# Pairs of heads in half-tiles of 64 partitions, 48 KB runs, three shared buffers

## The chip, the cores and the metric

The kernel runs on one core of one Trainium2 chip. The metric is the device time of one execution in microseconds: the median of three runs of the kernel before is 527.67 us (526.96 to 527.71). A profile of one further execution shows where the time goes.

## The reference

One step of decoding in a transformer block with a parallel feed-forward part: x has 4 rows (batch B = 4, one token each) of D = 640.

```python
def _A_ref(x, k_cache, v_cache, wq, wo):
    W = min(4096, max(256, Sk // 4))                     # Sk = 8192, so W = 2048
    q = (x @ wq).reshape(B, Sq, Hq, Dh).transpose(0, 2, 1, 3)   # 32 heads of 192
    k = k_cache[:, :, Sk - W:, :]
    v = v_cache[:, :, Sk - W:, :]
    scores = jnp.einsum("bhqd,bhkd->bhqk", q, k) * (Dh ** -0.5)
    p = _softmax(scores, axis=-1)
    o = jnp.einsum("bhqk,bhkd->bhqd", p, v)
    return o.transpose(0, 2, 1, 3).reshape(B, Sq, Hq * Dh) @ wo
def _B_ref(x, w1, w3, w2):                               # F = 1536
    return (silu(x @ w1) * (x @ w3)) @ w2
xn = _layernorm(x)
return x + _A_ref(xn, ...) + _B_ref(xn, ...)
```

All arrays are bf16. The last 2,048 positions of K and of V are read for each of 32 heads and 4 batch rows: 2 x 100.7 MB. wq and wo have 7.9 MB each, w1, w3 and w2 2.0 MB each. In all 223 MB are read, each byte once, for one query row per head and batch row.

## The kernel before

**Layout.** A tile of K or V holds one head for all four batch rows. `cache_rows` (L102) cuts the 2,048 positions into NQ = 32 pieces of NJ = 64; partition q*4 + b holds piece q of batch row b, which is one run of 64 x 192 x 2 B = 24 KB in memory. So a tile is 128 partitions x 24 KB, 3 MB, loaded by one DMA (`load_k` L105, `load_v` L110). K and V have three buffers each, 144 KB per partition in all. All large loads are issued by SyncE (SP), in the order in which they are written.

**Scores.** q is made once (L205 to L213) from wq, which is loaded into the V buffers in rows of 24 KB, and spread over the partitions by a matmul with a selector (`q_bcast`, L215). A slot s is half a head, 32 positions per partition. `mult` (L225) multiplies K with q on VectorE, `adder` (L234) sums the 192 products in groups of 16 by 12 identity matmuls that accumulate in PSUM, and `reduce_tile` (L248) finishes the sums on VectorE.

**Softmax and P·V.** The chain runs once for a pair of heads (u): `chain_lmax` takes the maximum of each partition, `chain_tr` transposes, `chain_gmax` takes that of each batch row and head, `chain_bc` spreads it back and ScalarE takes the exponential with its sum; `chain_z` (L288) writes the probabilities into a block form with a column for each batch row. `pv` (L303) does P·V of one head: 8 steps of 8 positions, in each three matmuls for three thirds of the head's 192 columns, with 32 columns of weights each. The result holds the wanted numbers on a diagonal; `pick` (L318) multiplies it with a mask, `pick_sum` (L327) sums it, `fold` (L333) adds the partitions by a small matmul, and ScalarE scales by the reciprocal of the softmax sum into o_bf.

**Output.** For a group of HG = 4 heads `ge_tr` (L346) transposes o_bf and `ge_proj` (L353) multiplies with that group's wo rows, accumulating in one PSUM tile for the whole kernel. A group's wo is one DMA of 0.98 MB in runs of 7.7 KB, double-buffered (`wo_load`, L115). w1, w3 and w2 go into K buffers after the last K (`ffn_load` L363, `w2_load` L368); `ffn_mm` (L375) does gate and up, `ffn_transpose` (L392) brings the product into the form that the last matmuls (L464 to L468) need.

**Order.** Every piece is entered with `add(slot, phase, ...)` (L400), and the pieces are written out sorted by slot and phase (L451). Each engine works in the order in which its instructions are written, apart from what a planner moves; `behind` (L244) holds VectorE's other work behind the multiplication of the same slot. The loads stand in the same list:

```python
        if j >= KBUFS:
            add(NC * j - 3, 0, load_k, j)
        add(NC * j + 2, 8, load_v, j)
        add(NC * j + L, 2, pv, j)
...
        add(a + 2 if not last else end, 10, wo_load, hg)
```

A load waits on SP until its buffer is free, and what is written behind it on SP waits with it.

Of the kernel before, what the change touches and what calls it, by code (L numbers as in the profile page):

```python
# [10 lines left out]
FP32 = mybir.dt.float32  # L11
# [7 lines left out]
def kernel(  # L19
# [14 lines left out]
    HG: int = 4,  # L34
    QP: int = 8,
    KBUFS: int = 3,
    VBUFS: int = 3,
    PBUFS: int = 2,
    L: int = 7,
    ALIGN: int = 144,  # L40
):

# [12 lines left out]
    NQ = P // B  # L55
    NJ = W // NQ
    NC = NJ // CH
    NK = Dh // DD
    SCALE = float(Dh) ** -0.5
    EPS = 1e-5  # L60
    MASK = -30000.0
    NS = H * NC
    HH = 2
    PL = 32 // B
    DV = 512 // PL
    NV = Dh // DV
    RPP = (HG * Dh) // P
    OW = HG * Dh
    NCH = 512
    QW = 512  # L70
    QB = QP * Dh // QW
    FC = F // P
    DH = D // 2
    assert NJ % CH == 0 and CH * DD <= 512 and QP * Dh % QW == 0
    assert OW % P == 0 and Dh % RPP == 0 and H % HG == 0 and HG % HH == 0 and H % QP == 0 and QP % HH == 0
    assert NV * 32 <= P and NJ % (2 * PL) == 0 and DV * NV == Dh
# [3 lines left out]
    NB = H * Dh // QW // NG  # L80
    assert H * Dh % (QW * NG) == 0 and NB <= 3
    assert DH <= 512 and F % NCH == 0 and NF <= NG

    const = ctx.enter_context(tc.tile_pool(name="const", bufs=1))
    kpool = ctx.enter_context(tc.tile_pool(name="kt", bufs=KBUFS))
    vpool = ctx.enter_context(tc.tile_pool(name="vt", bufs=VBUFS))
    wpool = ctx.enter_context(tc.tile_pool(name="wstream", bufs=2))
    ppool = ctx.enter_context(tc.tile_pool(name="pr", bufs=PBUFS))
    qpool = ctx.enter_context(tc.tile_pool(name="qbc", bufs=2))
    opool = ctx.enter_context(tc.tile_pool(name="o", bufs=2))  # L90
    small = ctx.enter_context(tc.tile_pool(name="small", bufs=3))
# [5 lines left out]
    kts, vts, prs, pss, scs, zts = {}, {}, {}, {}, {}, {}  # L97
    qbcs, wos, o_pss, rss, rcps, o_rs, o_bfs, chs = ({} for _ in range(8))
    mult_insts, es, o_ms = {}, {}, {}
    ORDER_DEP = mybir.DependencyInfo(mybir.DependencyClass.NoSync, mybir.DependencyReason.SCHED_ONLY)  # L100

    def cache_rows(cache, h):  # L102
        return cache[:, h, Sk - W:Sk, :].rearrange("b (q n) d -> q b (n d)", q=NQ)

    def load_k(j):  # L105
        kt = kpool.tile([P, NJ, Dh], BF16, tag="kt")
        nc.sync.dma_start(out=kt[:], in_=cache_rows(A_k_cache, j))
        kts[j] = kt

    def load_v(j):  # L110
        vt = vpool.tile([P, NJ, Dh], BF16, tag="vt")
        nc.sync.dma_start(out=vt[:], in_=cache_rows(A_v_cache, j))  # L112
        vts[j] = vt

    def wo_load(hg):  # L115
        wt = wpool.tile([P, RPP * D], BF16, tag="w")
        nc.sync.dma_start(out=wt[:], in_=A_wo[hg * OW:(hg + 1) * OW, :].rearrange("(p i) n -> p (i n)", i=RPP))
        wos[hg] = wt

    x_sb = ppool.tile([B, D], BF16, tag="pr")  # L120
    x_rows = A_x.rearrange("b s d -> (b s) d")
    nc.scalar.dma_start(out=x_sb[:], in_=x_rows)
# [7 lines left out]
    RV = NJ * Dh // (H * Dh)  # L130
    wq_rows = A_wq.rearrange("(p kc) n -> p kc n", kc=KC)
    wqs = []
    for r0 in range(0, KC, RV):
        r1 = min(r0 + RV, KC)
        wt = vpool.tile([P, RV, H * Dh], BF16, tag="vt")
        nc.sync.dma_start(out=wt[:, 0:r1 - r0, :], in_=wq_rows[:, r0:r1, :])  # L136
        wqs.append(wt)
    for h in range(KBUFS):
        load_k(h)
# [6 lines left out]
    nc.vector.memset(pad[:, 0:1], 0.0)  # L146
    nsc = const.tile([HH, HH], FP32, name="nsc")
    nc.vector.tensor_scalar_mul(out=nsc[:], in0=idf[0:HH, 0:HH], scalar1=-SCALE)
    selm = const.tile([P, B], FP32, name="selm")
    nc.vector.tensor_reduce(out=selm[:], in_=idf[:].rearrange("p (q b) -> p b q", b=B), axis=AX.X, op=ALU.add)  # L150
    selb = const.tile([P, B], BF16, name="selb")
    nc.vector.tensor_copy(out=selb[:], in_=selm[:])
    row = const.tile([P, 32], FP32, name="row")
    nc.vector.tensor_reduce(out=row[:], in_=idf[:].rearrange("p (g c) -> p c g", g=NG), axis=AX.X, op=ALU.add)
    fsel = const.tile([P, NV, B], FP32, name="fsel")
    nc.vector.tensor_reduce(out=fsel[:], in_=idf[:, 0:NV * 32].rearrange("p (k l b) -> p k b l", k=NV, l=PL), axis=AX.X, op=ALU.add)
    diag = const.tile([P, HH, PL], FP32, name="diag")
    for hh in range(HH):
        nc.vector.tensor_reduce(out=diag[:, hh, :], in_=row[:].rearrange("p (l b) -> p l b", b=B), axis=AX.X, op=ALU.add)
    oTs = []  # L160
    for i in range(2):
        oT = const.tile([P, RPP, 32], BF16, name=f"oT{i}")
        nc.gpsimd.memset(oT[:], 0.0)
        oTs.append(oT)

    xf = ppool.tile([B, D], FP32, tag="pr")
    nc.vector.tensor_copy(out=xf[:], in_=x_sb[:])
    ssum = const.tile([B, 1], FP32, name="ssum")
    nc.vector.tensor_reduce(out=ssum[:], in_=xf[:], axis=AX.X, op=ALU.add)
    negmean = const.tile([B, 1], FP32, name="negmean")  # L170
    nc.vector.tensor_scalar_mul(out=negmean[:], in0=ssum[:], scalar1=-1.0 / D)
    xc = ppool.tile([B, D], FP32, tag="pr")
    nc.vector.tensor_scalar_add(out=xc[:], in0=xf[:], scalar1=negmean[:, 0:1])
    ssq = const.tile([B, 1], FP32, name="ssq")
    nc.scalar.activation(out=xf[:], in_=xc[:], func=ACTF.Square, accum_out=ssq[:])
# [6 lines left out]
    xn = ppool.tile([B, D], BF16, tag="pr")  # L182
    nc.vector.tensor_scalar_mul(out=xn[:], in0=xc[:], scalar1=rstd[:, 0:1])

    xnT_ps = ps_t.tile([P, KC, B], BF16, tag="t")
    for kc in range(KC):
        nc.tensor.transpose(out=xnT_ps[:, kc, :], in_=xn[:, kc:D:KC], identity=idb[0:B, 0:B])
# [3 lines left out]

    sel = const.tile([P, NQ, B], BF16, name="sel")
    nc.vector.tensor_copy(out=sel[:], in_=selm[:].unsqueeze(1).to_broadcast([P, NQ, B]))

# [3 lines left out]
    for k in range(NB):  # L198
        if k < 2:
            qp = ps_add.tile([P, QW], FP32, tag="ps")  # L200
        else:
            qt = ps_o.tile([P, HH, QW], FP32, tag="o_ps")
            qp = qt[:, 0, :]
        q_pss.append(qp)
    for kc in range(KC):  # L205
        for k in range(NB):
            for g in range(NG):
                off = (k * NG + g) * QW
                nc.tensor.matmul(q_pss[k][32 * g:32 * g + 32, :], lhsT=xnT[:, kc, :],  # L209
                                 rhs=wqs[kc // RV][:, kc % RV, off:off + QW], start=(kc == 0), stop=(kc == KC - 1))  # L210
    q_sb = const.tile([P, NB, QW], BF16, name="q_sb")
    for k in range(NB):
        nc.scalar.copy(out=q_sb[:, k, :], in_=q_pss[k][:, :])  # L213

    def q_bcast(qg, m):  # L215
        k, g = (qg * QB + m) // NG, (qg * QB + m) % NG
        if m == 0:
            qbc = qpool.tile([P, QP, Dh], BF16, tag="qbc")
            qbcs[qg] = qbc
        bp = ps_t.tile([P, QW], FP32, tag="t")  # L220
        nc.tensor.matmul(bp[:], lhsT=sel[32 * g:32 * g + B].rearrange("k q b -> k (q b)"),  # L221
                         rhs=q_sb[32 * g:32 * g + B, k, :], start=True, stop=True)
        nc.scalar.copy(out=qbcs[qg][:].rearrange("p h d -> p (h d)")[:, m * QW:(m + 1) * QW], in_=bp[:])  # L223

    def mult(s):  # L225
        j, c = s // NC, s % NC
        pr = ppool.tile([P, CH, Dh], BF16, tag="pr")
        mi = nc.vector.tensor_tensor(out=pr[:], in0=kts[j][:, c * CH:(c + 1) * CH, :],  # L228
                                     in1=qbcs[j // QP][:, j % QP, :].unsqueeze(1).to_broadcast([P, CH, Dh]),
                                     op=ALU.mult)  # L230
        prs[s] = pr
        mult_insts[s] = mi

    def adder(s):  # L234
        ps = ps_add.tile([P, CH, DD], FP32, tag="ps")
        pr = prs.pop(s)
        for kk in range(NK):
            nc.tensor.matmul(ps[:], lhsT=idb[:], rhs=pr[:, :, kk * DD:(kk + 1) * DD],  # L238
                             start=(kk == 0), stop=(kk == NK - 1))
        pss[s] = ps  # L240

    slot = [0]

    def behind(inst):  # L244
        if slot[0] in mult_insts:
            tc.add_manual_dep(inst.ins, mult_insts[slot[0]].ins.name, ORDER_DEP, reason="vector engine issue order")

    def reduce_tile(s):  # L248
        j, c = s // NC, s % NC
        if s % (HH * NC) == 0:  # L250
            sc = small.tile([P, HH, NJ], FP32, tag="sc", bufs=2)
            scs[j // HH] = sc
        ri = nc.vector.tensor_reduce(out=scs[j // HH][:, j % HH, c * CH:(c + 1) * CH], in_=pss.pop(s)[:], axis=AX.X, op=ALU.add)  # L253
        behind(ri)

    def chain_lmax(u):
        lmax = small.tile([P, HH], FP32, tag="lmax")
        behind(nc.vector.tensor_reduce(out=lmax[:], in_=scs[u][:], axis=AX.X, op=ALU.max))  # L258
        chs[u] = [lmax]
# [43 lines left out]
    def pv(j):  # L303
        u, hh = j // HH, j % HH
        if hh == 0:
            o_ps = ps_o.tile([P, HH, PL * DV], FP32, tag="o_ps")
            o_pss[u] = o_ps
# [196 lines left out]
```

## Time and profile before

| | |
|---|---|
| median of the runs | 527.67 us |
| the profiled execution | 526.79 us |
| its span, first to last instruction | 525.0 us |
| busy: TensorE, VectorE, ScalarE | 326.4, 328.3, 39.6 us |
| main DMA queue | 222.97 MB, 99.0% of 16 engines' span |
| granted TensorE clock, mean | 0.844 |

The page divides the span into 40 slices of 13.1 us; a digit is the busy share of a slice in tenths. "Idle before" of a group of instructions is the idle time of its engine just ahead of them, with what ended it. The chain of waits is followed back from the last instruction. In the timeline, a line gives start and length in us, then engine, line, operation, output and inputs, and how many. PEld is TensorE's loading of weights, which overlaps its matmuls. Matmuls that write different columns of the array run beside each other, so their mean lengths don't add up.

### The profile page before, as it was taken

Reading aid. Unit: us, or ns where it says so; the run is one execution under the profiler, and the core shown is the slowest. Engines: PE = TensorE matmul, PEld = TensorE weight load, DVE = VectorE, ACT = ScalarE, POOL = GpSimd, SP = SyncE. Lnnn points to the kernel's source line nnn. Section 1 sums busy time; section 2 is a strip of 40 time slices with the busy share of each in tenths; the row PEclk is TensorE's granted clock in tenths of the full one; section 3 lists DMA queues with packets and bytes.
Section 4 is the critical chain, followed back from the end, with each engine's and each line's share of the span. In section 5 each row is a group of like instructions: output and inputs, shape, how many; then the busy total and the mean of one; then the engine's idle time right before and its main releaser. Section 6 shows DMA issues by size and latency. Waiting matters only on the chain.

```text
span 525.0 us, 4658 instructions
## 1 busy us (share of the span) xinstructions
PE 326.4 (62%) x1991; PEld 142.2 (27%) x1991; DVE 328.3 (63%) x289; ACT 39.6 (8%) x121; POOL 1.8 (0%) x11
## 2 busy tenths in 40 slices
PE   2356376864758487662858566572857737585864
PEld 1122122321323133221324223231322313232432
DVE  3069455767757376865757486573758657575842
ACT  2300000100000010001000000100100000000121
POOL 1000000000000000000000000000000000000000
PEclk9999887786888778797878769797897868888889
DMA  8999999999999999999999999999999999999996
GB/s 360 433 436 428 431 436 426 438 426 433 431 432 432 433 434 427 436 429 429 439 424 434 429 435 426 438 422 439 434 430 429 430 434 434 430 433 430 426 428 256
DMA packets 11723, 223.25 MB, mean 425 GB/s; under 512 B 1316, under 2 KB 1464, under 8 KB 2872
## 3 DMA queue, kind: packets, MB, share of 16 engines
q1 hardware_dynamic: 11688, 222.97, 99.0%
q8 instruction: 15, 0.25, 0.2%
q14 instruction: 4, 0.03, 0.0%
q10 hardware_dynamic: 16, 0.01, 0.0%
HBM read 222.96 MB, written 0.01 MB: 425 GB/s over the span
## 4 chain that ended last, share of the span: by engine, by line
DMA 77%; DVE 13%; PE 8%; SPq 1%; issue 0%; DVEq 0%
DMA kt<-in_A_k_cache_dram 73%; DVE pr L228 11%; PE ps L238 6%; DMA w2t<-in_B_w_dram 5%; PE o_ps L313 1%; DVE sc L253 1%; SPq L112 0%; DVE o_r L331 0%; SPq L136 0%; DVE o_m L323 0%; PE acc L357 0%; SPq L372 0%; PE ft L467 0%; DVE z L291 0%; DVE res L470 0%
## 5 line engine op out<-in xcount | busy, mean ns | idle before, releaser
L238 PE MATMUL ps<-pr,idb 128*128 128x512 bf16 x768 | 223.7, 452 | 166.3 <-DVE pr L228 166.3
L228 DVE TENSOR_TENSOR pr<-kt,qbc 128x6144 bf16<-128x6144 bf16 x64 | 214.5, 3352 | 166.8 <-DMA kt<-in_A_k_cache_dram 166.8
L238 PEld LDWEIGHTS <-idb 128*128 128x128 bf16 x768 | 83.9, 112 | 285.1 <-issue 223.9
L313 PE MATMUL o_ps<-vt,z 128*32 128x512 bf16 x768 | 66.3, 389 | 1.2 <-DMA vt<-in_A_v_cache_dram 0.6
L253 DVE TENSOR_REDUCE sc<-ps 128x32 f32<-128x512 f32 x64 | 43.7, 683 | 6.8 <-PE ps L238 6.7
L313 PEld LDWEIGHTS <-z 128*32 128x32 bf16 x768 | 32.0, 98 | 28.3 <-issue 10.5
L331 DVE TENSOR_REDUCE o_r<-o_m 96x128 f32<-96x1024 f32 (+1 forms) x17 | 30.7, 1807 | 0.1
L283 ACT ACTIVATE e<-sc,negm 128x64 bf16<-128x64 f32 x32 | 10.9, 340 | 239.4 <-DVE negm L279 239.4
L323 DVE TENSOR_TENSOR o_m<-o_ps,diag 96x1024 f32<-96x1024 f32 (+1 forms) x17 | 19.5, 1148 | 7.6 <-PE o_ps L313 7.6
L344 ACT ACTIVATE o_bf<-fp,rcp 4x192 bf16<-4x192 f32 x32 | 11.4, 403 | 132.0 <-PE fp L338 132.0
L338 PE MATMUL fp<-o_r,fsel 96*4 96x128 f32 x96 | 13.1, 273 | 1.8 <-DVE o_r L331 1.8
L223 ACT CAST qbc<-bp 128x512 bf16<-128x512 f32 x12 | 6.8, 590 | 81.2 <-PE bp L221 81.2
L291 DVE TENSOR_TENSOR z<-e,selb 128x512 bf16<-128x512 bf16 x16 | 10.8, 678 | 0.9 <-ACT e L283 0.9
L209 PE MATMUL qp<-wt,xnT 128*32 128x512 bf16 x40 | 5.3, 623 | 8.2 <-DMA wt<-in_A_wq_dram 8.2
L338 PEld LDWEIGHTS fp<-o_r,fsel 96*4 96x4 f32 x96 | 7.1, 86 | 9.8 <-issue 5.5
L357 PE MATMUL acc<-wt,oT 128*32 128x320 bf16 x96 | 7.9, 301 | 0.8 <-DVE oT L351 0.8
L263 PE MATMUL mt<-idf,lmax 128*2 128x128 f32 x16 | 4.8, 301 | 5.5 <-DVE lmax L258 5.4
L277 PEld LDWEIGHTS mt<-nsc,gmq 2*128 2x128 f32 x32 | 4.7, 183 | 7.8 <-issue 6.4
L277 PE MATMUL mt<-nsc,gmq 2*128 2x2 f32 x32 | 6.1, 257 | 1.1 <-DVE gmq L271 1.1
L283 ACT ACTIVATION_READ_ACCUMULATOR e<-sc,negm 128x1 f32 x32 | 6.0, 187 | 0.0
L209 PEld LDWEIGHTS <-xnT 128*32 128x32 bf16 x60 | 2.4, 133 | 11.9 <-issue 11.0
L263 PEld LDWEIGHTS mt<-idf,lmax 128*2 128x2 f32 x16 | 1.3, 83 | 13.8 <-issue 8.1
(65 smaller groups left out, 69.9 us busy)
## 6 DMA issues: line engine op xcount, KB each, us to landing
kt<-in_A_k_cache_dram SPq DMA_DIRECT2D x32, 3072.0 KB, 34.3
vt<-in_A_v_cache_dram SPq DMA_DIRECT2D x32, 3072.0 KB, 32.4
wt<-in_A_wo_dram SPq DMA_DIRECT2D x8, 960.0 KB, 26.4
wt<-in_A_wq_dram SPq DMA_DIRECT2D x2, 3072.0 KB
wt<-in_B_w_dram SPq DMA_DIRECT2D x2, 1920.0 KB, 20.5
wt<-in_A_wq_dram SPq DMA_DIRECT2D x1, 1536.0 KB, 19.9
w2t<-in_B_w_dram SPq DMA_DIRECT2D x2, 640.0 KB
w2t<-in_B_w_dram SPq DMA_DIRECT2D x1, 480.0 KB
```

The costliest lines, as they stand in the source:

```text
L228: mi = nc.vector.tensor_tensor(out=pr[:], in0=kts[j][:, c * CH:(c + 1) * CH, :], in1=qbcs[j // QP][:, j % QP, :].unsqueeze(1).to_broadcast ...
L238: nc.tensor.matmul(ps[:], lhsT=idb[:], rhs=pr[:, :, kk * DD:(kk + 1) * DD], start=(kk == 0), stop=(kk == NK - 1))
L253: ri = nc.vector.tensor_reduce(out=scs[j // HH][:, j % HH, c * CH:(c + 1) * CH], in_=pss.pop(s)[:], axis=AX.X, op=ALU.add)
L277: nc.tensor.matmul(mt[:, P:P + HH], lhsT=gmq[:].rearrange("o q b -> o (q b)"), rhs=nsc[:], start=True, stop=True)
L283: nc.scalar.activation(out=e[:, hh, :], in_=sc[:, hh, :], func=ACTF.Exp, bias=negm[:, hh:hh + 1], scale=SCALE, accum_out=rs[:, hh:hh + 1])
L291: behind(nc.vector.tensor_tensor(out=z[:].rearrange("p h j b -> p (h j) b"), in0=e[:].rearrange("p h j -> p (h j)").unsqueeze(2).to_broadc ...
L313: nc.tensor.matmul(o_ps[32 * k:32 * k + 32, hh, :], lhsT=z[:, hh, g * PL:(g + 1) * PL, :].rearrange("p l b -> p (l b)"), rhs=vt[:, g * PL: ...
L323: behind(nc.vector.tensor_tensor(out=o_ms[u][:, h0:h1].rearrange("r h l d -> r (h l) d"), in0=o_pss[u][0:NV * 32, h0:h1, :].rearrange("r h ...
L331: behind(nc.vector.tensor_reduce(out=o_rs[u][:, h0:h1, :], in_=o_ms[u][:, h0:h1].rearrange("r h l d -> r h d l"), axis=AX.X, op=ALU.add))
L338: nc.tensor.matmul(fp[:, :, k * DV:(k + 1) * DV], lhsT=fsel[0:NV * 32, k, :], rhs=o_r[:], start=True, stop=True)
L344: nc.scalar.mul(out=o_bfs[hg][:, pr + hh, :], in_=fp[:, hh, :], mul=rcp[:, hh:hh + 1])
L357: nc.tensor.matmul(acc[32 * t:32 * t + 32, :], lhsT=oT[:, i, :], rhs=wo_t[:, i * D + t * DH:i * D + (t + 1) * DH], start=(hg == 0 and i == ...
```

## The change

A unit u is now a pair of heads (X = 2), 16 units in all. The 2,048 positions are cut into NQ = 16 pieces of NJ = 128, so a partition holds one run of 128 x 192 x 2 B = 48 KB. The first head of the pair lies in partitions 0 to 63, the second in 64 to 127; each half is loaded by its own DMA of 3 MB (`load`). A K or V tile is 6 MB, and there are three such buffers that K, V, the first four fifths of wq, and later w1, w3 and w2 together use in turn.

A unit has four slots, as two heads had before, with the same multiplications and identity matmuls. The softmax chain and everything behind it runs once per unit, as before once per pair. P·V has 64 columns of weights: 16 steps; the first two thirds of the columns are two matmuls beside each other into one PSUM bank (`pv(u, 0)`), the last third goes alternately to two halves of the second bank (`pv(u, 1)`). The output weights come in groups of 8, 8, 8, 4 and 4 heads, in runs of 15 KB for the groups of eight, into one buffer that the last two groups share; the transposes before the projection are matmuls with a selector, which also adds the two half-rows. w2 is loaded in runs of 10, 3.8 and 1.3 KB. VectorE and TensorE now follow the written order completely (`dve`, `pe`).

```diff
-    KBUFS: int = 3,
-    VBUFS: int = 3,
-    PBUFS: int = 2,
+    GS: tuple = (8, 8, 8, 4, 4),
     L: int = 7,
...
-    NQ = P // B
+    X = 2
+    HP = P // X
+    NQ = HP // B
...
-    kpool = ctx.enter_context(tc.tile_pool(name="kt", bufs=KBUFS))
-    vpool = ctx.enter_context(tc.tile_pool(name="vt", bufs=VBUFS))
-    wpool = ctx.enter_context(tc.tile_pool(name="wstream", bufs=2))
+    kvpool = ctx.enter_context(tc.tile_pool(name="kv", bufs=3))
+    wpool = ctx.enter_context(tc.tile_pool(name="wstream", bufs=1))
...
+    def load(cache, u):
+        kv = kvpool.tile([P, NJ, Dh], BF16, tag="kv")
+        for x in range(X):
+            nc.sync.dma_start(out=kv[x * HP:(x + 1) * HP],
+                              in_=cache[:, X * u + x, Sk - W:Sk, :].rearrange("b (q n) d -> q b (n d)", q=NQ))
+        return kv
...
+    def wo_load(g):
+        n = GS[g] * Dh // P
+        if g < len(GS) - 1:
+            wt = wpool.tile([P, GM * Dh // P * D], BF16, tag="w")
+            wos["tile"] = wt
+        at = 0 if g < len(GS) - 1 else GS[-2] * Dh // P * D
+        wos[g] = wos["tile"][:, at:at + n * D]
+        nc.sync.dma_start(out=wos[g], in_=A_wo[starts[g] * Dh:(starts[g] + GS[g]) * Dh, :].rearrange("(p i) n -> p (i n)", i=n))
...
+    def pv(u, bank):
+        if bank == 0:
+            o_ps = ps_o.tile([P, 2, PL * DV], FP32, tag="o_ps")
             o_pss[u] = o_ps
-        o_ps = o_pss[u]
-        z, vt = zts[u], vts.pop(j)
-        GN = NJ // PL
+        o_ps, z, vt = o_pss[u], zts[u], vts[u]
         for g in range(GN):
-            for k in range(NV):
...
+            for k in range(2) if bank == 0 else (2,):
+                t = k if bank == 0 else g % 2
+                pe(nc.tensor.matmul(o_ps[t * HP:(t + 1) * HP, bank, :], lhsT=z[:, g * PL:(g + 1) * PL, :].rearrange("p l c -> p (l c)"),
+                   rhs=vt[:, g * PL:(g + 1) * PL, k * DV:(k + 1) * DV],
+                   start=(g < bank + 1), stop=(g >= GN - 1 - bank)))
...
     def ffn_load(which):
-        wt = kpool.tile([P, KC, F], BF16, tag="kt")
-        nc.sync.dma_start(out=wt[:], in_={1: B_w1, 3: B_w3}[which].rearrange("(p kc) n -> p kc n", kc=KC))
-        ffn[which] = wt
...
+        if which == 1:
+            ft = kvpool.tile([P, NJ, Dh], BF16, tag="kv")
+            ffn["tile"] = ft[:].rearrange("p j d -> p (j d)")
+        at = which // 2 * KC * F
+        ffn[which] = ffn["tile"][:, at:at + KC * F].rearrange("p (kc n) -> p kc n", kc=KC)
+        nc.sync.dma_start(out=ffn[which], in_={1: B_w1, 3: B_w3}[which].rearrange("(p kc) n -> p kc n", kc=KC))
...
+    def w2_load(i0, i1):
+        if i0 == 0:
+            ffn[2] = ffn["tile"][:, 2 * KC * F:2 * KC * F + NF * CF * D].rearrange("p (i n) -> p i n", n=D)
+        nc.sync.dma_start(out=ffn[2][:, i0:i1, :], in_=B_w2.rearrange("(p i) n -> p i n", p=P)[:, i0:i1, :])
...
         for kc in range(KC):
+            rows = ffn[which][:, kc, :].rearrange("p (f n c) -> p f n c", n=NF, c=CF)
             for n in range(NF):
-                nc.tensor.matmul(gt[32 * n:32 * n + 32, :], lhsT=xnT[:, kc, :],
-                                 rhs=ffn[which][:, kc, n * NCH:(n + 1) * NCH],
-                                 start=(kc == 0), stop=(kc == KC - 1))
+                pe(nc.tensor.matmul(gt[32 * n:32 * n + 32, :], lhsT=xnT[:, kc, :], rhs=rows[:, :, n, :], start=(kc == 0), stop=(kc == KC - 1)))
...
+    for u in range(U):
+        n, fin = NC * (u + 1), u == U - 1
+        if u >= 2:
+            add(NC * u - NC, 20, load_k, u)
+        add(NC * u + NC - 1 if not fin else NC * u, 21, load_v, u)
+        add(n, 5, chain_lmax, u)
+        add(n, 6, chain_tr, u)
+        add(n, 9, chain_gmax, u)
+        add(n + 1, 2, chain_bc, u)
+        add(n + 1, 4.5, chain_exp, u)
+        add(n + 1, 10, chain_z, u)
+        add(n + 2, 2, rowsum, u)
+        add(n + 2, 5, rcp, u)
+        v = NC * u + L
+        add(v, 2, pv, u, 0)
+        add(v + 1, 2, pv, u, 1)
...
+        add(v + 3, 2, fold, u)
+    free = [NC]
+    for g in range(len(GS)):
+        t = NC * ((starts[g] + GS[g]) // X - 1) + L + 4
+        add(t, 2, ge_tr, g)
+        add(t, 4, ge_copy, g)
+        add(t + 1, 2, ge_proj, g)
+        if g < len(GS) - 1:
+            add(free[-1], 22, wo_load, g)
+        free.append(t + 1)
+    f = NC * (U - 1) + L
+    add(end - 1, 23, ffn_load, 1)
+    add(end - 1, 24, ffn_load, 3)
+    add(end - 1, 25, wo_load, len(GS) - 1)
+    for i0, i1 in ((0, (NF - 1) * CF), ((NF - 1) * CF, NF * CF - 1), (NF * CF - 1, NF * CF)):
+        add(end - 1, 26, w2_load, i0, i1)
     add(end // 2, 0, x_load)
-    add(end + 4, 0, ffn_mm, 1)
-    add(end + 9, 0, ffn_mm, 3)
-    add(end + 10, 0, ffn_transpose)
+    add(f + 2, 1, ffn_mm, 1)
+    add(f + 4, 3, ffn_mm, 3)
+    add(f + 4, 5, ffn_transpose)
```

## The prediction, made before the result was known

> **What bounds the kernel now.** I read the page's 40 slices first, then the DMA queues, the chain that ended last, the stretches and, for the end, the timeline. Slices and queues:
>
> ```profile
> DVE  3069455767757376865757486573758657575842
> DMA  8999999999999999999999999999999999999996
> GB/s 360 433 436 428 431 436 426 438 426 433 431 432 432 433 434 427 436 429 429 439 424 434 429 435 426 438 422 439 434 430 429 430 434 434 430 433 430 426 428 256
> DMA packets 11723, 223.25 MB, mean 425 GB/s; under 512 B 1316, under 2 KB 1464, under 8 KB 2872
> ...
> q1 hardware_dynamic: 11688, 222.97, 99.0%
> ```
>
> The transfer engines are busy in every slice while VectorE is about two thirds busy; one queue carries nearly all. The chain and two waits say the same:
>
> ```profile
> DMA 77%; DVE 13%; PE 8%; SPq 1%; issue 0%; DVEq 0%
> ```
>
> ```profile
> DVE pr L228 <- DMA kt<-in_A_k_cache_dram: 166.8, 30, 20.1
> PE ps L238 <- DVE pr L228: 166.3, 34, 9.6
> ```
>
> VectorE waits 166.8 us for keys and TensorE waits for VectorE. The 13% of VectorE in the chain is no limit: those pieces lie between a release and an issue while earlier transfers still run. By stretches (columns: length, busy time of PE, PEld, DVE, ACT, POOL, then clock, DMA share, GB/s):
>
> ```profile
> 140.00:240.00 100.00, 67.28 (x387) 29.08 (x386) 65.11 (x56) 6.09 (x21) 0.00 (x0) 0.83 1.01 432
> 340.00:440.00 100.00, 63.78 (x413) 28.80 (x412) 65.41 (x53) 6.22 (x22) 0.00 (x0) 0.84 1.01 432
> 500.00:525.00 25.00, 14.48 (x152) 7.12 (x152) 8.82 (x18) 5.17 (x12) 0.00 (x0) 0.93 0.80 337
> ```
>
> So until the last landing the time is bytes over 432 GB/s, with no gap to win. The records of single packets in the same trace show what is left inside the stream: a 24,576 B packet takes 912 ns, 15,360 B 573 ns, 7,680 B 291 ns, 5,120 B 196 ns. Slope between the first two is 0.0368 ns per byte, so about 8 ns of each packet does not depend on size. The end:
>
> ```profile
> 504.54 3.54 PE L313 MATMUL o_ps<-vt,z 128*32 128x512 bf16 x24 [0.53 <-DVE z L291]
> ...
> 510.43 1.91 PE L313 MATMUL o_ps<-vt,z 128*32 128x512 bf16 x24 [0.62 <-DMA vt<-in_A_v_cache_dram]
> ...
> 517.57 0.99 PE L357 MATMUL acc<-wt,oT 128*32 128x320 bf16 x12
> 518.26 0.10 PEld L467 LDWEIGHTS <-hT 128*32 128x32 bf16 x1
> 518.61 0.48 DVE L457 CAST attn_bf<-acc 64x320 bf16<-64x320 f32 x1 [0.57 <-PE acc L357]
> ...
> 521.31 0.72 PE L467 MATMUL ft<-w2t,hT 128*32 128x320 bf16 x8 [0.42 <-DMA w2t<-in_B_w_dram]
> 521.31 0.50 PEld L467 LDWEIGHTS <-hT 128*32 128x32 bf16 x7 [0.64 <-issue]
> 522.07 0.48 DVE L470 TENSOR_TENSOR res<-ft,attn_bf 64x320 bf16<-64x320 f32 x1 [2.63 <-PE ft L467]
> ```
>
> The last w2 piece lands at 521.27 and the result is added at 522.55, 1.28 us later. The attention chain from the last V (510.43) to the projection's end (518.56) lasts 8.1 us and has 2.7 us to spare.
>
> The profiled execution took 526.79 us for a span of 525.0 us; the median of the runs is 527.67, which is 0.88 above it. I sum against 526.79 and add 0.88 at the end.
>
> **The change, part by part.**
>
> K and V runs. Bytes stay. 8,192 packets of 24,576 B become 4,096 of 49,152 B, if a run stays one packet. A packet of 49,152 B is then 2 x 912 - 8 = 1,816 ns. Saved: 4,096 x 8 ns / 16 engines = 2.1 us. Bounds: 0 (runs cut as before) to 2.1.
>
> Output weights. 1,024 packets of 291 ns become 384 of 573 ns (three groups of eight heads) and 256 of 291 ns (two of four): 298.0 to 294.5 us of engine time, /16 = 0.2 us. w2 goes from 256 x 196, 128 x 149 and 128 x 55 ns to runs of 10,240 B (385 ns by the slope), 3,840 and 1,280 B: 76.3 to 75.4 us, /16 = 0.05 us. Together the stream shrinks by 2.35 us. The number of K and V issues stays 64 (two per unit, 0.54 us each on SP, which is idle most of the time); wo has 5 for 8.
>
> Half the partitions. The trace has no large transfer to 64 partitions. Both halves of a tile are queued one behind the other, and each engine moves four runs of each. Bounds from the nearest rows: nothing, if an engine's 912 ns is its own limit; 912 ns more per 24 KB, if two engines must share one way in while all of them write the same half: 8,192 x 912 / 16 = +467 us. I take nothing, because the nearest row, the 912 ns of a long packet, is flat whatever the other fifteen engines do at that moment; the other end is a rival.
>
> [...]
>
> Three buffers in turn. V of unit u takes the buffer of K of unit u, K of u+2 that of V of u-1. From the rows, a unit (two heads, 6.3 MB, two times 14.55 us of stream) costs VectorE from the landing of K: four multiplications of 3.35, four row sums of 0.68, lmax 0.28, pick 1.21, gmax and gmq 0.49, pick_sum 1.91, z of 1,024 elements about 1.2 (512 take 0.68), less overlaps of 0.1 each: the last multiplication ends about 20.6 us after the landing. The queue runs dry 29.1 us after it, when the V before and the next K are in: 8.5 us to spare, 6 when 2.5 us are allowed for the issue and the start (the first issue is at 0.73 us, and the first 2 us show a DMA share of 0.45). V is freed when P·V is through, about 31 us after K landed, and its buffer is wanted at 43.6. So nothing is added; without that cover each microsecond short costs up to 14 us over 14 units. wo with one buffer waits for the projection of the group before, which TensorE reaches at the head of the same slot; SP has V and K of the next units behind it, with these 6 us of cover. wq, K0 and K1 go out with no wait; V0 waits for the q matmuls (about 22 us, K1 lands at 49): nothing.
>
> Start. K0 lands whole at about 34.5 instead of 28.8 us; VectorE, two thirds loaded, takes it up. Nothing at the end.
>
> The tail. After the last V come w1, w3, wo and w2 (6.88 MB), where before came w3, wo and w2 (4.92 MB), so the last landing is 4.6 us further behind it, 15.4 us against 10.9. But a V now holds two heads. From its landing: P·V is 16 + 8 steps of two matmuls (three ran in 0.24 us fast, 0.43 slow: the 24 matmuls of the two rows above took 1.91 and 3.54). With 3.4 us at the slow pace, as at 504.54, it ends at 6.9, without at 5.2. Two picks and two sums (0.69 + 1.02 each), the first pair beside the second bank: 8.7. The gate's matmuls (15 in 1.25) now stand in TensorE's written order behind P·V, so cast 0.58, table load 1.28 and Silu 0.63 end at about 10.7, and only then ScalarE scales the fold (0.71): 11.4. Transposes 0.7 with their hand-over, the up matmuls 1.3, cast, product and transposes 1.6, projection 1.0: 15.8. Then the 24 matmuls of w2 (3 x 0.72) and the sum (0.48): 18.4 after the V. Before, the end was 10.9 + 1.28 = 12.2 after it. So the last add comes 18.4 - 15.4 = 3.0 us after the last landing, against 1.28: +1.7 us. At the fast pace +0.05. z of the last unit may also be late: in my count VectorE finishes it between 1 us before and 1.6 us after the V lands, which makes the upper end +3.4. I take +1.1: nearest to the slow P·V row at 504.54, since TensorE is idle before, but partly warm from the adders shortly before the V.
>
> Sum: 526.79 - 2.35 + 1.1 = 525.5, plus 0.88: 526.4 us.
>
> **The rivals.**
>
> A, the forecast: stream shorter by 2.35, tail +0 to +1.3. 525.3 to 526.6, with 0.5 of scatter below: 524.8 to 526.8. For it: flat packets and a share of 99.0% leave the time to the packets.
>
> B, the tail takes it back: attention, gate and up chain set the end instead of the w2 landing. Place: after the last V; price +1.3 to +4.5 (late z, slow P·V, a gate whose strided operand reads slower by up to 1.3 us): 526.6 to 529.8. It decides from +2.35 on. For it: 2.7 us to spare become less than none in the sum above. Against: the DMA after V grew by 4.6 us.
>
> C, runs are cut and the change does not do what it says for packets: 0.25 saved, tail as in A or B: 527.4 to 530. Against: 24 KB runs travel uncut.
>
> D, other side: the halves collide. Place: every K and V transfer; up to +467 us, so up to about 990 us. It is slower than before as soon as the mean 24 KB takes over 0.5% more than 912 ns (2.35 of 467 us). For it: the completions of the engines come within 0.7 to 1.9 us of each other at each transfer, so all write the same half at once. Against: no row shows engines hindering each other.
>
> E, buffers come free too late: dry stream in each unit. 1 to 2 us short in 14 units: 530 to 555 us. It decides when a unit holds K for more than 27 us instead of 20.6. Against: VectorE's 65 of 100 us.
>
> **How the numbers follow.** A 0.45; B 0.25 (0.17 within 0.2%, 0.08 slower); C 0.07 (0.03 and 0.04); D 0.13; E 0.10. 0.2% is 1.06 us, about what a measurement tells from no change. Faster 0.45, same 0.20, slower 0.35. Predicted 526.4. The range runs from 524.2 (whole saving, tail 0.5 shorter, scatter 0.6) to 535, which takes in B, C and the mild half of E; D and the rest of E, 0.18, stay out. A's own range is 524.8 to 526.8.
>
> **What would show it.** In the page of the changed kernel: about 6,900 packets in the main queue and GB/s slices near 434 for the stream; K and V issues of 3,072 KB, landing times like now; slices of 9 throughout. A 49,152 B packet of 1.8 us says A, of 3.6 us D. Gaps in the DMA slices in the middle, with SP waiting for mult or P·V while nothing is in flight, would show E. In the tail, what released the last w2 matmuls: the landing (A) or the projection (B). The prediction is wrong if long packets have a price of their own, in HBM or in SBUF, or if the halves cost anything.

## The result: 1.94 times slower

| | before | after |
|---|---|---|
| median | 527.00 us | 1,027.53 us |
| ratio, with its 95% interval | | 1.943 (1.932 to 1.954) |
| the profiled execution | 526.79 us | 1,015.03 us |
| its span | 525.0 us | 1,013.0 us |
| granted TensorE clock, mean | 0.844 | 0.692 |

Two of the six runs of the changed kernel (1,033.5 and 1,035.1 us) fell in a slower state, and the ratio leaves them out.

The forecast was 526.4 us in a range up to 535; the time is that of rival D, the collision of the halves, to which I had given 0.13, and lies some 37 us above even the 990 that D allowed.

Slices and queues of the changed kernel, as on the page of before:

```profile
DVE  1056034080431607053080622508034070713422
DMA  9999999999999999999999999999999999999995
GB/s 373 214 195 214 218 251 204 213 216 214 215 208 208 216 215 214 214 245 216 214 212 210 215 212 214 212 203 254 216 210 215 214 213 216 217 216 221 214 210 246
DMA packets 7052, 223.27 MB, mean 220 GB/s; under 512 B 1252, under 2 KB 1400, under 8 KB 1784
...
q1 hardware_dynamic: 7016, 222.97, 99.0%
```

Three lines are to be read together. The bytes are the same and the packets are fewer, as the change says. The DMA row is full in all slices but the last, so the queue does not run dry. Yet the rate is 373 GB/s in the first slice, while wq is loaded, and about 214 from the first K on. An engine that is "busy" 99% of the time is not one that moves at its rate: the digit is a 9 at about 432 GB/s before as at 214 here, and can't tell a packet that flows from one that is held up. In the records, a packet of 49,152 B takes 3,697 ns on average (median 3,754), where two of 24,576 B took 1,824.

The waits (who waited for whom: us in total, times, longest):

```profile
DVE pr L245 <- DMA kv<-in_A_k_cache_dram: 558.5, 16, 44.4
```

VectorE waits 558.5 us for K instead of 166.8. In time: the records put the stream, from the first large packet to the last of w2, at 1,003.9 us instead of 519.6 (+484.2). From the end of the last w2 packet to the start of the output's last packet it is 5.9 instead of 2.1 us (+3.7). Together that is 487.9 of the 488.2 us that lie between the two profiled executions.

### The profile page after: what moved, and what is told of

It reads as the page before. It is cut to its first block, busy times and chain, and to the rows that moved or that the text cites. A ratio compares the mean times of both kernels' runs of the same rounds, so it can differ in the third digit from the quotient of the medians.

```text
span 1013.0 us, 4671 instructions
## 1 busy us (share of the span) xinstructions
PE 394.9 (39%) x2015; PEld 169.0 (17%) x2015; DVE 338.0 (33%) x288; ACT 37.3 (4%) x102; POOL 1.7 (0%) x10
## 4 chain that ended last, share of the span: by engine, by line
another core or an unknown queue 56%; DVE 24%; PE 14%; DMA 5%; issue 0%; ACT 0%; SPq 0%; DVEq 0%; ACTq 0%
DVE pr L245 16%; PE ps L254 9%; DMA kv<-in_A_k_cache_dram 5%; PE o_ps L319 3%; DVE o_r L336 3%; DVE sc L261 2%; DVE z L295 2%; DVE gmax L275 0%; DVE gmq L277 0%; PE mt L270 0%; PE gp L358 0%; PE ft L483 0%; PE gt L391 0%; PE acc L368 0%
## 5 line engine op out<-in xcount | busy, mean ns | idle before, releaser
L254 PE MATMUL ps<-pr,idb 128*128 128x512 bf16 x768 | 236.0, 467 | 423.1 <-DVE pr L245 423.0
L245 DVE TENSOR_TENSOR pr<-kv,qbc 128x6144 bf16<-128x6144 bf16 x64 | 213.8, 3342 | 558.5 <-DMA kv<-in_A_k_cache_dram 558.5
L319 PE MATMUL o_ps<-kv,z 128*64 128x512 bf16 x768 | 121.1, 481 | 169.4 <-DMA kv<-in_A_v_cache_dram 169.4
L319 PEld LDWEIGHTS <-z 128*64 128x64 bf16 x768 | 54.4, 137 | 238.3 <-issue 139.4
L336 DVE TENSOR_REDUCE o_r<-o_m 128x128 f32<-128x1024 f32 (+1 forms) x17 | 30.3, 1781 | 0.1
L328 DVE TENSOR_TENSOR o_m<-o_ps,diag 128x1024 f32<-128x1024 f32 (+1 forms) x17 | 19.6, 1153 | 20.7 <-PE o_ps L319 20.7
L295 DVE TENSOR_TENSOR z<-e,selb 128x1024 bf16<-128x1024 bf16 x16 | 19.3, 1205 | 0.6 <-ACT e L290 0.6
L351 ACT ACTIVATE o_bf<-fp,r 8x192 bf16<-8x192 f32 x32 | 11.4, 404 | 32.4 <-PE tb L301 32.4
L345 PE MATMUL fp<-o_r,fsel 128*8 128x64 f32 x96 | 8.4, 223 | 3.9 <-DVE o_r L336 3.2
L270 PE MATMUL mt<-idf,lmax 128*1 128x128 f32 x16 | 6.5, 409 | 0.0
```

The source lines that it names most:

```text
L245: dve(nc.vector.tensor_tensor(out=pr[:], in0=kts[u][:, c * CH:(c + 1) * CH, :], in1=qbcs[u // X][:, u % X, :].unsqueeze(1).to_broadcast([P ...
L254: pe(nc.tensor.matmul(pss[s][:], lhsT=idb[:], rhs=prs[s][:, :, kk * DD:(kk + 1) * DD], start=(kk == 0), stop=(kk == NK - 1)))
L270: pe(nc.tensor.transpose(out=mt[0:1, 0:P], in_=chs[u][0][:], identity=idf[:]))
L295: dve(nc.vector.tensor_tensor(out=z[:], in0=es.pop(u)[:].unsqueeze(2).to_broadcast([P, NJ, C]), in1=selb[:].unsqueeze(1).to_broadcast([P, ...
L319: pe(nc.tensor.matmul(o_ps[t * HP:(t + 1) * HP, bank, :], lhsT=z[:, g * PL:(g + 1) * PL, :].rearrange("p l c -> p (l c)"), rhs=vt[:, g * P ...
L328: dve(nc.vector.tensor_tensor(out=o_ms[u][:, b0:b1].rearrange("r k l d -> r (k l) d"), in0=o_pss[u][:, b0:b1, :].rearrange("r k (l d) -> r ...
```

## The experiments

Theory 1 is that the engines hinder each other when all of them write the same half of the partitions. The expectations picture it as two engines that share a way into a half; that picture is a supposition, which no record shows. The rivals: long runs (or their distance in memory) are slow by themselves (theory 2); three buffers in turn starve the stream (theory 3); 64 partitions are slow wherever they lie (theory 4); halves serialize whatever the order (theory 5).

### The halves alone, in the kernel before

```diff
-        nc.sync.dma_start(out=kt[:], in_=cache_rows(A_k_cache, j))
+        for x in range(2):
+            nc.sync.dma_start(out=kt[64 * x:64 * x + 64], in_=cache_rows(A_k_cache, j)[NQ // 2 * x:NQ // 2 * x + NQ // 2])
```

(the same for V)

> The kernel before with one thing of the change alone: each load of K or V is cut into two DMAs, partitions 0 to 63 and 64 to 127, runs of 24 KB as before. Theory 1: packets of 24 KB go from 912 to about 1,850 ns and the kernel to 990 to 1,030 us. Theory 2 (run length) and theory 3 (three buffers in turn): 527 to 530 us, 64 more issues of 0.54 us on SP being hidden.

Measured: 1,004.74 us (two executions, 997.5 and 1,012.0), ratio 1.905 (1.893 to 1.918). Its slices:

```profile
DMA  9999999999999999999999999999999999999996
GB/s 364 208 218 229 215 211 219 210 232 214 216 211 238 213 217 220 213 233 218 215 218 219 233 219 218 218 218 235 220 218 219 234 220 219 220 217 221 217 251 220
```

The 24 KB packets take 1,789 ns on average (median 1,851) instead of 912. Run length, number of heads per tile, buffers and order are those of before. Theories 2 and 3 fall as explanations of the slowdown: cutting a load in halves is enough.

### Loads alone, in stages

A kernel of loads only, three buffers of 48 KB, where a small copy on VectorE marks each landing. The stages differ in the partitions that a load goes to and in the length of its runs:

```diff
+        nc.sync.dma_start(out=kv[:, 0:NJ // 2 * Dh], in_=rows(h, W, 32))            # full24
+        nc.sync.dma_start(out=kv[0:64], in_=rows(h, W, 16))                         # low48
+        nc.sync.dma_start(out=kv[32:96], in_=rows(h, W, 16))                        # mid48
+        nc.sync.dma_start(out=kv[0:64, 0:NJ // 2 * Dh], in_=rows(h, W // 2, 16))    # low24, 1.5 MB
+        nc.sync.dma_start(out=kv[0:64], in_=vrows(h, W, 16))                        # both
+        nc.sync.dma_start(out=kv[64:128], in_=vrows(h + 1, W, 16))
...
+        nc.sync.dma_start(out=kv[64:96], in_=A_v_cache[:, 0, 0:W // 2, :].rearrange("b (q n) d -> q b (n d)", q=8))   # shift, then both again
```

> Loads alone, in stages one behind the other, with one small VectorE copy per landing and zeros as output; nothing of the reference is computed. Time per 3 MB. Theory 1: 128 partitions in 24 KB runs 7.3 us; partitions 0 to 63 in 48 KB runs 14.8; partitions 32 to 95 in 48 KB runs 7.3, since they reach both halves; 0 to 63 in 24 KB runs 7.4 per 1.5 MB (14.8 per 3 MB); 128 partitions in 48 KB runs 7.3; lower and upper half in turn 14.8; the same from two queues between 7.3 and 14.8; and, after one transfer that only engines 0 to 7 carry and that takes them 7.3 us, lower and upper half in turn at about 7.3, since then one group of engines writes the lower half while the other writes the upper. Theory 2, long runs are slow: 14.8 for every stage with 48 KB runs and 7.3 for both with 24 KB. Theory 4, 64 partitions are slow wherever they lie: 14.8 also for 32 to 95 and after the shift.

The timeline of VectorE (start, length, what, idle before it): the distance between two starts is the time of one load. In the order of the lines: full24, low48, mid48, one DMA of 6 MB to all 128 partitions in 48 KB runs, both, and both after the shift, two landings each.

```profile
18.19 0.16 DVE L52 COPY sink<-kv 128x1 bf16<-128x1 bf16 x1 [7.08 <-DMA kv<-in_A_k_cache_dram]
25.49 0.16 DVE L52 COPY sink<-kv 128x1 bf16<-128x1 bf16 x1 [7.14 <-DMA kv<-in_A_k_cache_dram]
...
92.93 0.15 DVE L52 COPY sink<-kv 64x1 bf16<-64x1 bf16 x1 [15.18 <-DMA kv<-in_A_k_cache_dram]
108.26 0.15 DVE L52 COPY sink<-kv 64x1 bf16<-64x1 bf16 x1 [15.19 <-DMA kv<-in_A_k_cache_dram]
...
199.40 0.31 DVE L52 COPY sink<-kv 32x1 bf16<-32x1 bf16 x2 [6.96 <-DMA kv<-in_A_k_cache_dram]
206.68 0.31 DVE L52 COPY sink<-kv 32x1 bf16<-32x1 bf16 x2 [6.97 <-DMA kv<-in_A_k_cache_dram]
...
335.09 0.16 DVE L52 COPY sink<-kv 128x1 bf16<-128x1 bf16 x1 [29.53 <-DMA kv<-in_A_v_cache_dram]
365.31 0.16 DVE L52 COPY sink<-kv 128x1 bf16<-128x1 bf16 x1 [30.07 <-DMA kv<-in_A_v_cache_dram]
...
441.14 0.15 DVE L52 COPY sink<-kv 64x1 bf16<-64x1 bf16 x1 [14.67 <-DMA kv<-in_A_v_cache_dram]
456.33 0.15 DVE L52 COPY sink<-kv 64x1 bf16<-64x1 bf16 x1 [15.03 <-DMA kv<-in_A_v_cache_dram]
...
711.21 0.15 DVE L52 COPY sink<-kv 64x1 bf16<-64x1 bf16 x1 [7.17 <-DMA kv<-in_A_v_cache_dram]
718.55 0.15 DVE L52 COPY sink<-kv 64x1 bf16<-64x1 bf16 x1 [7.19 <-DMA kv<-in_A_v_cache_dram]
```

| stage | time of 3 MB | packet |
|---|---|---|
| 128 partitions, 24 KB runs | 7.30 us | 912 ns |
| 0 to 63, 48 KB | 15.33 | 3,840 |
| 32 to 95, 48 KB | 7.27 | 1,815 to 1,820 |
| 0 to 63, 24 KB | 15.3 (7.66 per 1.5 MB) | 1,920 |
| 128 partitions, 48 KB, one DMA with 16 pieces outermost | 15.1 (30.2 per 6 MB) | 3,829 |
| lower and upper half in turn, 48 KB | 15.2 | 3,838 |
| the same from two queues (SP and ScalarE) | 15.0 | 3,831 |
| the same after the shift | 7.34 | 1,820 to 1,900 |

Low48 and mid48 differ in nothing but 32 partitions of offset: the same number of partitions, runs and bytes, from other heads of the same cache. One takes 15.33 us, the other 7.27. That ends theories 2 and 4. The last row ends theory 5: the halves in turn take 7.34 us, about as long as full24 (7.30), once eight of the engines are one half-transfer behind (the shift, of 1.5 MB, took 7.37 us), so that one group writes the lower half while the other writes the upper. What was slow is not the half but that all engines wrote it at once (15.2 us). Two queues didn't help: at 15.0 us they come out just beyond the slow end of my open range of 7.3 to 14.8. The one DMA to all 128 partitions is a miss, 15.1 us for an expected 7.3; the next two experiments come back to it.

The last of the sixteen halves after the shift took 14.85 us again (from 814.23 to 829.08): the leading group had gone on to the next load, one to all 128 partitions, whose 24 KB packets took 1,858 ns on average until then. So the load to all partitions behind the halves cost the lagging group a half at the slow pace.

### One DMA for a whole tile

A unit pairs heads u and u + 16, so that batch row and head have one common step in memory; the selectors follow, and wo's runs become 7.7 and 3.8 KB.

```diff
-        for x in range(X):
-            nc.sync.dma_start(out=kv[x * HP:(x + 1) * HP],
-                              in_=cache[:, X * u + x, Sk - W:Sk, :].rearrange("b (q n) d -> q b (n d)", q=NQ))
+        nc.sync.dma_start(out=kv[:], in_=cache[:, u:u + U + 1:U, Sk - W:Sk, :].rearrange("b x (q n) d -> q (b x) (n d)", q=NQ))
```

> The changed kernel, but a unit pairs heads u and u+16, so that batch row and head merge into one stride and each K or V tile is one DMA to all 128 partitions, still in runs of 48 KB through the same three buffers (wo then comes in runs of 7.7 and 3.8 KB). Theory 1, two engines share a way into one half of the partitions: 48 KB packets fall from 3,697 to about 1,816 ns, the stream to about 517 us, and the kernel takes 525 to 529 us, with what the tail costs on top of 2.2 us saved. Theory 2, long runs or their distance in memory are slow by themselves: packets stay near 3,700 ns and the kernel near 1,027 us. Theory 3, three buffers in turn starve the stream: packets of 1,816 ns, but gaps in the DMA slices and well over 530 us.

Measured: 1,031.81 us, ratio 1.956 (1.954 to 1.959), packets of 3,759 ns. A miss: I had taken 128 partitions in one DMA for the cure. Read alone, this run speaks for theory 2, as its expectation says. But mid48 moves the same 48 KB runs in 1,815 ns, so the length is not it. What one DMA and two halves have in common is the cut of the memory side: 16 pieces outermost, as many as there are engines. But this load also takes two heads that lie 50 MB apart in memory, and the run does not part the two.

### How a load is cut, and how much of a lead is needed

```diff
+        nc.sync.dma_start(out=kv[:, 0:NJ // 2 * Dh], in_=A_v_cache[:, u:u + 17:16, Sk - W // 2:Sk, :].rearrange("b x (q n) d -> q (b x) (n d)", q=16))   # outer16
+        nc.sync.dma_start(out=kv[:, 0:NJ // 4 * Dh], in_=A_v_cache[:, u, Sk - W // 2:Sk, :].rearrange("b (q n) d -> q b (n d)", q=32))   # outer32
+        nc.sync.dma_start(out=kv[:, 0:NJ // 2 * Dh], in_=A_v_cache[0:2, u, 0:2 * W, :].rearrange("b (q n) d -> q b (n d)", q=64))   # outer64
...
+        nc.sync.dma_start(out=kv[64:96, 0:n * Dh], in_=A_v_cache[:, 0, 0:8 * n, :].rearrange("b (q n) d -> q b (n d)", q=8))   # shift by 24 KB or 12 KB packets
```

> Loads alone again (zeros as output, nothing of the reference), with all engines brought level between the stages. To 128 partitions, 24 KB runs, the memory side cut with 16 pieces outermost (each engine gets 8 neighbouring partitions): theory 1 expects 1,850 to 1,930 ns a packet and 14.8 us per 3 MB, as in the one-DMA kernel; with 32 pieces outermost (12 KB runs) 460 ns and 3.7 us per 1.5 MB; with 64 outermost 912 ns if the cut deals partitions so that no two engines share a way in at once, else 1,850. Then halves of 64 partitions in turn after a shift of 3.65 us (half of a half-transfer) and of 1.84 us (a quarter): if the lead w is kept and only the time in the same half is doubled, a 3 MB half takes 14.8 - w, so 11.0 to 11.5 and 12.8 to 13.4 us. If a shift must be whole to help: 14.8 in both; if any shift frees it: 7.3 in both.

All of the first three go to 128 partitions. With 16 pieces outermost 3 MB take 14.9 us and a 24 KB packet mostly 1,918 ns; with 64 outermost 7.31 us and 916 ns; with 32 outermost, in 12 KB runs, 3.69 us per 1.5 MB and 465 ns. So the load to all partitions was slow too when its source had 16 pieces outermost (14.9 us), and the kernel before, fast, has 32 (packets of 912 ns). The lines of two landings with 16 pieces:

```profile
122.19 0.16 DVE L52 COPY sink<-kv 128x1 bf16<-128x1 bf16 x1 [14.76 <-DMA kv<-in_A_v_cache_dram]
137.11 0.16 DVE L52 COPY sink<-kv 128x1 bf16<-128x1 bf16 x1 [14.76 <-DMA kv<-in_A_v_cache_dram]
```

That the cut is the reason is argued and not shown. The 8 neighbouring partitions for each engine, in the expectation, fit the shift of the loads alone, whose 8 pieces outermost went at half the rate (1.5 MB in 7.37 us), but which engine writes which partition is not in the records. And the load with 16 pieces is also the only one of the three that takes two heads 50 MB apart, a rival that no run tries alone.

The partial shifts gave 14.0 us per half after the one of 3.65 us, and 15.1 after the one of 1.84. I had expected 11.0 to 11.5 and 12.8 to 13.4. The records of the packets tell why: most of the shift was lost before the halves began. Of the two loads that bring the engines level, the second went out behind the shift, only at 254.65 us, when its one buffer was free, and eight of the sixteen engines stood still from 253.9 to 256.1 us. After the first shift the two groups of eight engines then finished a half about 1.4 us apart (279.6 to 280.0 and 281.1 to 281.3 us), and so in each later half; after the second, fifteen engines finished within 0.8 us and one a microsecond later, so hardly a lead was left. My expectation was a fixed time less the lead; with the measured 15.2 for it, it gives 13.8 for the first (measured 14.0) and 15.2 for the second (15.1), but 7.9 for the whole shift (7.34): it holds within 0.6 us, no better. The first lead was kept through all twelve halves.

### The changed kernel with a shift

```diff
+    def shift():
+        kv = kvpool.tile([P, NJ, Dh], BF16, tag="kv")
+        nc.sync.dma_start(out=kv[HP:HP + 32], in_=A_k_cache[:, 0, 0:W // 2, :].rearrange("b (q n) d -> q b (n d)", q=8))
+        early[1] = kv
```

> The changed kernel with one load more: ahead of K0, 32 runs of 48 KB of no use go to partitions 64 to 95 of K1's buffer, cut so that engines 0 to 7 alone carry them, four packets each (7.3 us). Everything else stays. Theory 1 (two engines that share a way in hinder each other only while both write the same half): engines 0 to 7 are from then on one half-transfer behind, packets fall from 3,697 to about 1,830 ns, and the kernel takes 532 to 540 us: 527 less 2.2 for the long runs, plus 7.3 for the extra packets, plus what the tail costs, with some us more if three buffers can't hold the shift everywhere. Theory 5, halves serialize whatever the order: 1,030 to 1,045 us.

Measured: 951.69 us, ratio 1.807 (1.804 to 1.810). Slices, then stretches (length, busy PE, PEld, DVE, ACT, POOL, clock, DMA share, GB/s):

```profile
GB/s 401 428 402 303 306 420 354 224 214 203 226 205 203 222 227 212 216 209 213 210 213 213 210 212 207 241 210 212 211 211 212 209 207 218 207 211 220 207 290 39
```

```profile
124.00:150.00 26.00, 12.47 (x68) 5.56 (x68) 6.31 (x6) 0.00 (x0) 0.00 (x0) 0.74 1.01 422
150.00:160.00 10.00, 7.04 (x32) 2.90 (x31) 9.96 (x8) 1.69 (x5) 0.00 (x0) 0.83 0.95 385
160.00:166.00 6.00, 5.51 (x24) 2.13 (x25) 5.06 (x5) 0.29 (x1) 0.00 (x0) 0.72 0.76 262
166.00:176.00 10.00, 6.91 (x50) 3.03 (x47) 0.00 (x0) 0.00 (x0) 0.00 (x0) 1.00 0.90 192
176.00:200.00 24.00, 10.56 (x43) 4.51 (x43) 18.77 (x15) 1.50 (x5) 0.00 (x0) 0.74 1.07 226
```

The shift works at first: over 400 GB/s but for two slices around the first wo load (303 and 306), and 422 again from 124 to 150 us, with median packets of 1,815 ns and the two groups' completions 7.5 us apart. Then half of the engines run dry; in the records about 8 to 11 of 16 are busy from 158 to 166 us. The reason stands in the timelines of SP and of VectorE:

```profile
139.27 1.17 SPq L126 DMA_DIRECT2D kv<-in_A_k_cache_dram  x2
164.39 1.17 SPq L126 DMA_DIRECT2D kv<-in_A_v_cache_dram  x2
```

```profile
144.24 3.36 DVE L255 TENSOR_TENSOR pr<-kv,qbc 128x6144 bf16<-128x6144 bf16 x1 [19.40 <-DMA kv<-in_A_k_cache_dram]
...
161.04 3.33 DVE L255 TENSOR_TENSOR pr<-kv,qbc 128x6144 bf16<-128x6144 bf16 x1
```

K landed at 144.24 (its first multiplication), the fourth multiplication ends at 164.37, and V, which takes that buffer, is issued at 164.39: 20.2 us after the landing, as my sum had it (20.6). The cover of 6 us that I counted is less than the lead of 7.3. The leading group waits for the issue, the groups go on together (fifteen engines finish the next half within 1.4 us of each other, one a load later), and from then to the end packets take about 3,700 ns again. So the expectation was right that a lead frees the halves (422 GB/s while it held) and wrong that three buffers would hold it.

### The halves of the kernel before, with a shift

The edit of the first experiment, and one load of 32 runs of 24 KB ahead of K0 that is meant for eight of the engines alone.

```diff
+        nc.sync.dma_start(out=kt[64:96], in_=A_k_cache[:, 0, 0:W // 4, :].rearrange("b (q n) d -> q b (n d)", q=8))
```

> The kernel before with its loads cut into halves of 64 partitions (24 KB runs, as in the earlier run of about 1,004 us), and one load of no use ahead of K0: 32 runs of 24 KB to partitions 64 to 95 of K2's buffer, which engines 0 to 7 alone carry, four packets each, 3.65 us. Theory 1: from then on one group of engines writes the lower half while the other writes the upper, and the six buffers of 3 MB (some 34 us from issue to landing) keep the queue full, so that the lead is not lost as it was with three buffers: packets of 912 to 960 ns, 530 to 537 us, that is 527 plus 3.65 and some us for meetings at wo and the weights. If the lead is lost midway, as with three buffers: 700 to 1,000 us, with the packets doubling from one moment on. Theory 5, halves serialize whatever the order: 1,000 to 1,010 us.

Measured: 691.4 to 761.0 us in four executions, against 1,004.74 without the shift. Slices of one of 736.5 us:

```profile
GB/s 373 419 369 313 396 378 344 298 381 391 328 235 354 358 362 250 291 364 293 267 221 245 268 274 302 238 248 302 318 331 249 256 333 332 347 360 271 202 260 74
```

One useless load of 0.8 MB saves some 240 to 310 us, which theory 5 doesn't allow; but it is not 530 to 537 either. The dips at slices 4, 8, 12 and 16 lie near the loads of wo. Its 7.7 KB packets take 578 ns at the median instead of 291, and between 200 and 220 us, beside them, the 24 KB packets of K and V take 1,691 ns at the median instead of 995 between 160 and 180. A wo load goes to all partitions; that the leading group meets there the one that still writes its half, as at the end of the loads alone (1,858 ns), is my reading. But the engines do not fall level: the sixteen completions of one load lie 4.4 us apart until 44 us, 20 us at 123 and up to 30 later. So the groups were scattered, not joined again; why the time is 691 us and more, and what wo alone costs, stays open.

### The rest of the change, without the halves

```diff
-            nc.sync.dma_start(out=kv[x * HP:(x + 1) * HP],
-                              in_=cache[:, X * u + x, Sk - W:Sk, :].rearrange("b (q n) d -> q b (n d)", q=NQ))
+            nc.sync.dma_start(out=kv[:, x * NJ // 2:(x + 1) * NJ // 2],
+                              in_=cache[:, X * u + x, Sk - W:Sk, :].rearrange("b (q n) d -> q b (n d)", q=2 * NQ))
```

> The changed kernel, but each of the two DMAs of a tile goes to all 128 partitions in runs of 24 KB (the first head into the first half of each partition's 48 KB, the second into the second half). Buffers, sizes, number and order of the loads, and all computation stay, so the time tells what the rest of the change costs; the rows of the two heads lie elsewhere than the computation takes them, so heads are mixed. Theory 1: 24 KB packets of 912 ns, no trace of the slow packets, 527 to 530 us: 0.25 us saved by wo and w2, +0 to +3.4 by the tail of my sum. Theory 3, three buffers in turn starve the stream: over 532 us, with gaps in the DMA slices. If the tail is as long as the upper end of the sum, the last add stands about 4.6 us after the last landing, else 1.3 to 3.

Measured: 528.76 us against 526.93, ratio 1.0039 (1.0026 to 1.0051). Slices, and the tail from the last V on:

```profile
DMA  8999999999999999999999999999999999999994
GB/s 359 427 436 427 439 425 436 429 436 424 442 419 444 421 442 424 436 427 436 427 436 431 433 431 432 433 427 432 432 431 435 431 433 432 429 424 442 429 424 201
```

```profile
503.38 6.81 PE L319 MATMUL o_ps<-kv,z 128*64 128x512 bf16 x48 [0.60 <-DVE z L295]
...
518.22 1.78 PE L368 MATMUL acc<-wt,oT 128*32 128x320 bf16 x12
...
520.33 3.30 PE L483 MATMUL ft<-ft,hT 128*32 128x320 bf16 x24 [0.32 <-DMA ft<-in_B_w_dram]
...
523.66 0.48 DVE L486 TENSOR_TENSOR res<-ft,t 64x320 bf16<-64x320 f32 x1 [2.77 <-PE ft L483]
```

The packets are back at 912 ns and no slice has a gap: the halves are nearly the whole effect, and three buffers in turn cost nothing at the normal rate. Most of what is left, +1.83 us, is the tail: from the end of the last w2 packet to the start of the output's last packet it is 3.58 us instead of 2.14 (+1.4). The stream is 519.8 against 519.6 us, so the 0.25 us of the longer wo and w2 runs does not show.

## Why the prediction was wrong, step by step

- **What bounds the kernel.** Right: the stream. VectorE has 338 us of work instead of 328, TensorE as many large matmuls, and the stream's time went straight into the total.
- **Half the partitions.** This is the step that failed. I bounded it from 0 to +467 us and took 0, "because the nearest row, the 912 ns of a long packet, is flat whatever the other fifteen engines do". But the row comes from loads to all partitions, which in the loads alone go at full rate as well (912 ns); it holds no case of all engines writing the same half. It could not speak to the question, and the other end of the bound stood equally near. That end was my estimate, twice 912 ns for engines that share a way in; no run shows such a way, only what the halves cost. Measured: +484 us in the stream; a packet of half a tile is not twice but 3,840 / 1,816 = 2.11 times as long when the engines are level, and 2.04 in the changed kernel, whose engines finish a load 0.7 us apart at the start and up to 5.6 us at the end. Why it is a little more than twice stays open.
- **Rival D.** Right in place, mechanism and mark: the packet of 3.6 us that it named is 3.70 on average. Its price was short by some 37 us. That the engines come within 0.7 to 1.9 us of each other at each transfer I had read from the first half of the trace of before alone; towards its end it is 3.2 us. What I had held against D, that no row shows engines hindering each other, was an absence of rows and not a row.
- **Long runs.** Right in itself: 1,815 to 1,820 ns where nothing collides, against 1,816 in the sum, so 2.1 us would be saved. No kernel here got it: both that had 48 KB runs in all partitions, in halves and in one DMA, were slow.
- **Three buffers in turn.** Right at the normal rate (no gap without the halves); the hold of K is 20.2 us against 20.6 in the sum. Under the shift the 6 us of cover were too few.
- **The tail.** Without the halves right in sign, a little small: +1.4 us against +1.1, within 0 to +3.4. In the changed kernel it is +3.7, just outside: w2's matmuls begin at 1,006.57 us, 0.95 us after its last packet, because the projection stands before them. P·V took 6.81 against 6.9; the projection (1.78 for 1.0) and w2's matmuls (3.30 for 2.2) ran at the slow pace, which I had given to P·V alone; the runs show the two paces and not what sets them. The gate's strided operand, to which rival B gave up to 1.3 us, cost 0.05: 15 matmuls took 1.30 us in the changed kernel and 1.25 before.
- **The sum without the halves.** 528.76 less the 2.1 us of long runs is an estimate of 526.7, 0.3 us under the 526.93 of before in that experiment, where the sum had -2.35 + 1.1 = -1.25. So even without the collision the change would not have been faster by more than a measurement tells: that part of the forecast was too hopeful by about 1 us.

## What to carry to other kernels

When a load is cut anew, ask which partitions all engines write at the same moment, not how many bytes or runs the load has: 64 partitions from 32 to 95 went at 432 GB/s and 64 from 0 to 63 at 205, and a load to all 128 partitions went at half rate too when its source had 16 pieces outermost and two heads. Halves laid at 32 to 95 and in the remaining partitions were not tried in the kernel. In the profiles here the mark was a DMA row of nines with half the GB/s (214 for 432) and packets of double length (3,697 ns for 1,816); the busy share alone, 99.0% in both kernels, showed nothing. And where the trace of before has no case of the thing in question, a flat row is no argument for the cheap end of a bound.

## What the runs showed of the hardware

- The engines drifted apart only slowly: the completions of one load lie 0.7 us apart at the start and 3.2 at the end of the kernel before, 0.7 and 5.6 in the changed kernel. That spread was no cure: the changed kernel's packets take 3,718 ns on average in the first 100 us and 3,663 between 900 and 1,000.
- A lead between two groups of eight was kept while they carried halves alone and the queue held work: 1.4 us through twelve halves, 7.3 through fifteen. In the kernel before with halves and a shift, where loads to all partitions lie in between, the engines came to lie up to 30 us apart.
- The price went with the lead: halves in turn cost 15.2 us per 3 MB when level, 14.0 with a lead of 1.4, 7.34 with one of 7.3.
- In the shifted kernel the leading group ran dry and lost its lead: one gap of some 8 us (158 to 166) was followed by about half the rate (213 GB/s from 300 to 900 us) to the end.
- Two queues instead of one did not part the engines (15.0 us per 3 MB against 15.2).
